# Channel mixing in five chunks of 464 tokens instead of six of 384, with results added in place

## The chip, the cores and the metric

The kernel runs on one core of a Trainium2 chip. The metric is device time in microseconds (us); the time before is the median of three runs. Engines: PE is TensorE (PEld its weight loads, which overlap with matmuls), DVE is VectorE, ACT is ScalarE, POOL is GpSimd, SP issues the transfers.

## The reference

Attention with a window of 64 comes first, then a gated spatial mixing, then a token and a channel mixing. The change touches only the last one. `_moe2_ref` is called with x of 4 x 576 x 512:

```python
def _moe2_ref(x, w_tok1, w_tok2, w_ch1, w_ch2):
    xt = x.transpose(0, 2, 1)
    h = np.maximum(xt @ w_tok1, 0.0) @ w_tok2
    u = x + h.transpose(0, 2, 1)
    h2 = np.maximum(u @ w_ch1, 0.0) @ w_ch2      # 512 -> 1536 -> 512
    return (u + h2).astype(np.float32)
```

## The kernel before

All 2,304 tokens (4 batches of 576) lie along the free axis of one tile U, 128 partitions x 4 x 2304, with the 512 features on partitions in four groups. Each product is made of three matmuls: both operands are split in a high and a low part (names ending in h and l), and high x high, high x low and low x high are summed (`mm3`, line 115 on).

The weights of both channel products come as 64-bit numbers. `load_wide` (line 93) fetches a tile into `wraw`; ACT takes a first step (line 106), DVE four (lines 107 to 111: L107, L109, L110, L111), ACT copies the high part (L112), POOL subtracts for the low part (L113). `wval` has two buffers, `wraw` three. There are 12 tiles c1 (512 x 128 each) and 12 tiles c2 (128 x 512 each). c1 of 0 to 6 and c2 of 0 to 2 are loaded while the token mixing runs; the other nine c2 and five c1 go to a pool `c2p`, which takes over memory that the token mixing uses until its end.

The token mixing runs batch by batch ahead of that: `x2nat` transposes U with PE (twenty transposes of 128 x 128 a batch, L407) into five PSUM tiles A, `tok1` makes two sums of 512 columns (hh and hl are their split, L419 and L420), `tok2` adds products of 288 columns to U (L431). PSUM has five tiles A and three tiles mm.

The channel mixing goes in chunks of CW = 384 tokens. `uin(c)` splits the chunk of U into uh (ACT, L476) and ul (DVE, L477), two buffers each. `ch1(u, ft)` makes hidden tile ft of 12: twelve matmuls of 384 columns into one mm tile (L123), then g3h (ACT, L486) and g3l (DVE, L487), four buffers each. `ch2(acc, g, ft)` adds it to four sums A, one for each output tile d, with three matmuls each (L497). ch1 is written one tile ahead of ch2. A chunk has 12 x 12 + 12 x 12 = 288 matmuls, each with a weight load. At its end DVE adds each sum and U into a tile `ot` (L532, four buffers), and SP sends it to outT (L533). The first three ch1 of chunk 0 are written between steps of the token mixing.

The order of instructions on each engine is the planner's outside the attention: it takes instructions by the order of the code and by its own estimate of when operands are ready; each engine then works its list in order.

Of the kernel before, what the change touches and what calls it, by code (L numbers as in the profile page):

```python
# [8 lines left out]
F32 = mybir.dt.float32  # L9
# [3 lines left out]
AF = mybir.ActivationFunctionType  # L13
ALU = mybir.AluOpType
# [5 lines left out]
P = 128  # L20
NTOK = B * S
# [6 lines left out]
def f(ap):  # L28
    return ap.bitcast(F32)
# [3 lines left out]
def tile_kernel(ctx, tc, qT, kT, kE, v, w_in, wsT, b_sp, w_out, w_t1, w_t2, w_c1, w_c2, mask, outT):  # L33

    nc = tc.nc

    def pool(name, side=None, stack=ctx, **kw):
        return stack.enter_context(tc.tile_pool(name=name, side=side, **kw))
# [10 lines left out]
    U = const.tile([P, 4, NTOK], F32, name="U")  # L49
# [65 lines left out]
    def mm3(o, steps, tail=()):  # L115

        todo = []
        for sh, sl, mh, ml in steps:
            todo += [(sh, mh), (sh, ml), (sl, mh)]
        todo += tail  # L120
        n = len(todo)
        for i, (a, c) in enumerate(todo):
            nc.tensor.matmul(o, a, c, start=(i == 0), stop=(i == n - 1))  # L123
# [5 lines left out]
    psmm = pool("psmm", bufs=3, space=PSUM)  # L129
# [234 lines left out]
    psA = pool("psA", bufs=5, space=PSUM)  # L364
# [69 lines left out]
    c1, c2 = {}, {}  # L434

    def load_c1(pl, ft):

        c1[ft] = [pl.tile([P, 4, 128], F32R, name=f"c1{x}{ft}") for x in "hl"]
        load_wide(lw, *[t.rearrange("p k c -> p (k c)") for t in c1[ft]],
                  w_c1[:, 128 * ft:128 * ft + 128].rearrange("(k p) c -> p k c", p=P), wmax=wmax)  # L440
# [26 lines left out]
    p3 = pool("p3", "left", stack=c_stack, bufs=1)  # L467
    wmax = DM
    lw = pool("lw3", "left", stack=c_stack, bufs=1)
    CW = 384  # L470

    def uin(c):
        t0 = CW * c
        uh = p3.tile([P, 4, CW], F32R, tag="uh", name="uh", bufs=2)
        ul = p3.tile([P, 4, CW], F32R, tag="ul", name="ul", bufs=2)
        nc.scalar.copy(out=uh, in_=U[:, :, t0:t0 + CW])  # L476
        nc.vector.tensor_tensor(out=ul, in0=U[:, :, t0:t0 + CW], in1=f(uh), op=ALU.subtract)  # L477
        return uh, ul

    def ch1(u, ft):  # L480
        uh, ul = u
        ps = psmm.tile([P, 512], F32, tag="mm", name="mm")
        mm3(ps[:, :CW], [(c1[ft][0][:, k, :], c1[ft][1][:, k, :], uh[:, k, :], ul[:, k, :]) for k in range(4)])
        gh = p3.tile([P, CW], F32R, tag="g3h", name="g3h", bufs=4)
        gl = p3.tile([P, CW], F32R, tag="g3l", name="g3l", bufs=4)
        nc.scalar.activation(out=gh, in_=ps[:, :CW], func=AF.Relu)  # L486
        nc.vector.scalar_tensor_tensor(out=gl, in0=ps[:, :CW], scalar=0.0, in1=f(gh), op0=ALU.max, op1=ALU.subtract)  # L487
        return gh, gl

    def ch2(acc, g, ft):  # L490
        gh, gl = g
        for d in range(4):
            dc = slice(128 * d, 128 * d + 128)
            wh, wl = c2[ft]
            todo = [(wh[:, dc], gh), (wl[:, dc], gh), (wh[:, dc], gl)]
            for i, (a, c) in enumerate(todo):
                nc.tensor.matmul(acc[d][:, :CW], a, c, start=(ft == 0 and i == 0), stop=(ft == 11 and i == 2))  # L497

    u0 = uin(0)
    tok2(1)  # L500
    tok1(2)
    x2nat(3)
    g0 = [ch1(u0, ft) for ft in range(2)]
    tok2(2)
    load_c1(p3, 4)
# [4 lines left out]
    load_c2(p3, 2)  # L510
    load_c1(p3, 6)
    g0.append(ch1(u0, 2))
    tok2(3)
    t_stack.close()
    r_stack.close()
    c2p = pool("c2p", "right", bufs=1)
    load_c2(c2p, 3)
    for k in range(4, 12):
        load_c2(c2p, k)
        if k < 9:  # L520
            load_c1(c2p, k + 3)
    for c in range(NTOK // CW):
        u = uin(c) if c else u0
        acc = [psA.tile([P, 512], F32, tag="A", name="A") for _ in range(4)]
        gq = [] if c else g0
        for ft in range(12):
            while len(gq) < min(ft + 2, 12):
                gq.append(ch1(u, len(gq)))
            ch2(acc, gq[ft], ft)
        for d in range(4):  # L530
            ot = c2p.tile([P, CW], F32, tag="ot", name="ot", bufs=4)
            nc.vector.tensor_tensor(out=ot, in0=acc[d][:, :CW], in1=U[:, d, CW * c:CW * c + CW], op=ALU.add)  # L532
            nc.sync.dma_start(out=outT[128 * d:128 * d + 128, CW * c:CW * c + CW], in_=ot)  # L533
    c_stack.close()


# [57 lines left out]
```

## Time and profile before

| what | value |
|---|---|
| median of three runs | 702.94 us (702.53 to 703.41) |
| the profiled execution, its own time | 704.92 us |
| its span, first to last instruction | 703.1 us |
| PE busy | 657.1 us, 93% of the span, 4,744 matmuls |
| DVE / ACT / POOL busy | 347.8 / 252.6 / 129.6 us |
| mean granted clock of PE | 0.982 |

The span is what lies between the core's first and last instruction; the execution's own time lies 1.8 us above it. Busy times are unions of records. A matmul's record overlaps with the next one's, so how fast matmuls follow each other is read from start times and counts.

### The profile page before, as it was taken

How to read it: one execution, taken by the hardware profiler on the slowest of the kernel's cores; microseconds unless marked ns; L12 is line 12 of the kernel's file. 1: busy time of each engine (PE TensorE's matmuls, PEld its weight loads, DVE VectorE, ACT ScalarE, POOL GpSimd, SP SyncE). 2: the span in 40 equal slices, each digit the busy share in tenths (PEclk: the TensorE clock that was granted, in tenths of full speed). 3: DMA queues.
4: the chain of work that ended last, by engine and by line, in shares of the span. 5: the costliest groups of instructions: out<-in, count | busy, mean ns of one | idle time of the engine just before them, and what ended most of it. 6: DMA issues, size and time to landing. Idle time of an engine off the chain costs nothing.

```text
span 703.1 us, 11915 instructions
## 1 busy us (share of the span) xinstructions
PE 657.1 (93%) x4744; PEld 627.7 (89%) x4744; DVE 347.8 (49%) x912; ACT 252.6 (36%) x675; POOL 129.6 (18%) x134
## 2 busy tenths in 40 slices
PE   2398899999999998899999998999999999999997
PEld 2387799899989898799998996999999999999996
DVE  4977576645574589921369689701311312212112
ACT  3667672553664353642345154301211111111110
POOL 2534410101220173632012143300000000000000
PEclk8589999999999999999999999999999999999999
DMA  8626552322240034100042234100100100100001
GB/s 287 199 78 186 182 170 69 116 90 68 84 151 2 1 104 129 60 1 1 1 150 91 89 121 150 45 1 1 46 1 0 46 1 1 46 0 13 34 1 45
DMA packets 27286, 50.24 MB, mean 71 GB/s; under 512 B 2784, under 2 KB 13408, under 8 KB 27232
## 3 DMA queue, kind: packets, MB, share of 16 engines
q1 hardware_dynamic: 27232, 49.49, 22.2%
q8 instruction: 37, 0.61, 0.4%
q14 instruction: 17, 0.14, 0.1%
HBM read 44.76 MB, written 4.72 MB: 70 GB/s over the span
## 4 chain that ended last, share of the span: by engine, by line
PE 75%; DVE 11%; DMA 6%; ACT 3%; issue 2%; POOL 1%; SPq 1%; DVEq 0%; POOLq 0%; ACTq 0%
PE mm L123 44%; PE A L497 20%; PE sc L184 3%; DVE wval L110 3%; PE A L123 3%; DMA kk<-in_kT 2%; PE xo L225 2%; DVE wval L111 2%; PE pt L213 2%; ACT pb L199 2%; DVE wval L107 1%; DMA raw<-in_wsT 1%; DMA U<-in_w_in 1%; DVE wval L109 1%; SPq L157 1%
## 5 line engine op out<-in xcount | busy, mean ns | idle before, releaser
L487 DVE SCALAR_TENSOR_TENSOR g3l<-mm,g3h 128x384 fp32r<-128x384 f32 x72 | 40.0, 557 | 191.0 <-ACT g3h L486 191.0
L486 ACT ACTIVATE g3h<-mm 128x384 fp32r<-128x384 f32 x72 | 35.3, 493 | 220.2 <-PE mm L123 220.1
L123 PE MATMUL mm<-uh,c1h 128*128 128x384 f32 x288 | 97.0, 337 | 1.2 <-ACT c1h L112 1.2
L497 PE MATMUL A<-g3h,c2l 128*128 128x384 f32 x288 | 97.2, 338 | 0.8 <-POOL c2l L113 0.8
L123 PE MATMUL mm<-uh,c1l 128*128 128x384 f32 x288 | 96.8, 337 | 1.2 <-POOL c1l L113 1.2
L123 PE MATMUL mm<-ul,c1h 128*128 128x384 f32 x288 | 96.7, 336 | 0.0
L497 PE MATMUL A<-g3l,c2h 128*128 128x384 f32 x288 | 94.1, 337 | 0.0
L497 PE MATMUL A<-g3h,c2h 128*128 128x384 f32 x288 | 93.7, 338 | 0.0
L199 ACT ACTIVATE pb<-pb,nm 128x128 f32<-128x128 f32 x144 | 55.9, 391 | 16.8 <-DVE nm L197 13.9
L184 PE MATMUL sc<-kk,QZ 128*64 128x128 f32 x576 | 39.7, 297 | 22.5 <-DMA kk<-in_kT 16.3
L184 PEld LDWEIGHTS sc<-kk,QZ 128*64 128x64 f32 x576 | 35.8, 152 | 23.2 <-issue 21.6
L123 PEld LDWEIGHTS mm<-uh,c1h 128*128 128x128 f32 x288 | 54.0, 188 | 1.9 <-ACT c1h L112 1.9
L123 PEld LDWEIGHTS mm<-uh,c1l 128*128 128x128 f32 x288 | 54.0, 188 | 1.9 <-POOL c1l L113 1.9
L497 PEld LDWEIGHTS A<-g3h,c2l 128*128 128x128 f32 x288 | 54.0, 187 | 1.5 <-POOL c2l L113 1.4
L497 PEld LDWEIGHTS A<-g3h,c2h 128*128 128x128 f32 x288 | 53.6, 187 | 0.6 <-ACT c2h L112 0.5
L123 PEld LDWEIGHTS mm<-ul,c1h 128*128 128x128 f32 x288 | 54.0, 188 | 0.0
L497 PEld LDWEIGHTS A<-g3l,c2h 128*128 128x128 f32 x288 | 53.8, 188 | 0.0
L123 PE MATMUL mm<-ws_h,nh 128*128 128x288 f32 x160 | 47.3, 300 | 1.9 <-DVE tmp L301 1.7
L123 PE MATMUL mm<-ws_l,nh 128*128 128x288 f32 x160 | 46.5, 295 | 0.0
L123 PE MATMUL mm<-gh,wo_h 128*128 128x288 f32 x128 | 38.2, 301 | 1.0 <-DVE tmp L301 0.8
L123 PE MATMUL mm<-gl,wo_h 128*128 128x288 f32 x128 | 38.1, 298 | 0.6 <-POOL gl L388 0.4
L194 DVE CUSTOM_DVE_ANT_0 pb<-sc,msk 128x128 f32<-128x128 f32 x144 | 33.4, 283 | 9.3 <-PE sc L184 9.3
(111 smaller groups left out, 1433.0 us busy)
## 6 DMA issues: line engine op xcount, KB each, us to landing
wraw<-in_w_c SPq DMA_DIRECT2D x24, 512.0 KB, 3.5
kk<-in_kT SPq DMA_DIRECT2D x16, 384.0 KB, 4.2
QZ<-in_qT SPq DMA_DIRECT2D x36, 128.0 KB, 4.1
va<-in_v SPq DMA_DIRECT2D x18, 256.0 KB, 3.1
vb<-in_v SPq DMA_DIRECT2D x18, 256.0 KB, 4.0
outT<-ot SPq DMA_DIRECT2D x24, 192.0 KB, 2.0
U<-in_w_in SPq DMA_DIRECT2D x8, 512.0 KB, 5.6
raw<-in_w_out SPq DMA_DIRECT2D x8, 256.0 KB, 3.6
```

The costliest lines, as they stand in the source:

```text
L107: nc.vector.tensor_scalar(out=x, in0=x, scalar1=TINY, scalar2=None, op0=ALU.max)
L110: nc.vector.scalar_tensor_tensor(out=xi, in0=high, scalar=-0x40000000, in1=xi, op0=ALU.bitwise_and, op1=ALU.bitwise_or)
L111: nc.vector.scalar_tensor_tensor(out=xi, in0=low, scalar=29, in1=xi, op0=ALU.logical_shift_right, op1=ALU.bitwise_or)
L123: nc.tensor.matmul(o, a, c, start=(i == 0), stop=(i == n - 1))
L184: nc.tensor.matmul(sc[64 * q:64 * q + 64, h, :], qz[:, h % 2, j, 64 * q:64 * q + 64], kk[:, j, step * q:step * q + 128], start=True, stop= ...
L194: nc.vector.tensor_tensor_reduce(out=half[:, h, :], in0=scs[g][:, h, :], in1=mk, scale=1.0, scalar=-3e38, op0=ALU.add, op1=ALU.max, accum_ ...
L199: nc.scalar.activation(out=half[:, h, :], in_=half[:, h, :], func=AF.Exp, scale=SCALE, bias=nm[:, h:h + 1], accum_out=sm[:, h:h + 1])
L213: nc.tensor.transpose(pt[:, h, :], pb[:, 4 * g + h, :], ident)
L225: nc.tensor.matmul(xo[64 * e:64 * e + 64, j, 64 * q:64 * q + 64], vt[q][:, hc], PT[:, 2 * j + e, 64 * q:64 * q + 64], start=True, stop=True)
L486: nc.scalar.activation(out=gh, in_=ps[:, :CW], func=AF.Relu)
L487: nc.vector.scalar_tensor_tensor(out=gl, in0=ps[:, :CW], scalar=0.0, in1=f(gh), op0=ALU.max, op1=ALU.subtract)
L497: nc.tensor.matmul(acc[d][:, :CW], a, c, start=(ft == 0 and i == 0), stop=(ft == 11 and i == 2))
```

## The change

CW becomes 464, so the 2,304 tokens fall into four chunks of 464 and one of 448; tiles are cut to a chunk's width w. A chunk's sums are added to U in place and sent from U, and the tiles `ot` go. In the last chunk, the products of the last three hidden tiles (9 to 11) are written after the others, output tile by output tile, each followed by its add and its transfer. Everything else is as it was.

```diff
-    CW = 384
+    CW = 464
 
     def uin(c):
         t0 = CW * c
+        w = min(CW, NTOK - t0)
         uh = p3.tile([P, 4, CW], F32R, tag="uh", name="uh", bufs=2)
         ul = p3.tile([P, 4, CW], F32R, tag="ul", name="ul", bufs=2)
-        nc.scalar.copy(out=uh, in_=U[:, :, t0:t0 + CW])
-        nc.vector.tensor_tensor(out=ul, in0=U[:, :, t0:t0 + CW], in1=f(uh), op=ALU.subtract)
+        uh, ul = uh[:, :, :w], ul[:, :, :w]
+        nc.scalar.copy(out=uh, in_=U[:, :, t0:t0 + w])
+        nc.vector.tensor_tensor(out=ul, in0=U[:, :, t0:t0 + w], in1=f(uh), op=ALU.subtract)
         return uh, ul
...
-    def ch2(acc, g, ft):
+    def ch2(acc, g, ft, ds=range(4)):
         gh, gl = g
-        for d in range(4):
+        for d in ds:
...
-    for c in range(NTOK // CW):
+    chunks = range(-(-NTOK // CW))
+    for c in chunks:
         u = uin(c) if c else u0
-        acc = [psA.tile([P, 512], F32, tag="A", name="A") for _ in range(4)]
+        w = u[0].shape[-1]
+        acc = [psA.tile([P, 512], F32, tag="A", name="A")[:, :w] for _ in range(4)]
         gq = [] if c else g0
+
+        late = 9 if c == chunks[-1] else 12
         for ft in range(12):
             while len(gq) < min(ft + 2, 12):
                 gq.append(ch1(u, len(gq)))
-            ch2(acc, gq[ft], ft)
+            if ft < late:
+                ch2(acc, gq[ft], ft)
         for d in range(4):
-            ot = c2p.tile([P, CW], F32, tag="ot", name="ot", bufs=4)
-            nc.vector.tensor_tensor(out=ot, in0=acc[d][:, :CW], in1=U[:, d, CW * c:CW * c + CW], op=ALU.add)
-            nc.sync.dma_start(out=outT[128 * d:128 * d + 128, CW * c:CW * c + CW], in_=ot)
+            for ft in range(late, 12):
+                ch2(acc, gq[ft], ft, (d,))
+            ts_ = slice(CW * c, CW * c + w)
+            nc.vector.tensor_tensor(out=U[:, d, ts_], in0=acc[d], in1=U[:, d, ts_], op=ALU.add)
+            nc.sync.dma_start(out=outT[128 * d:128 * d + 128, ts_], in_=U[:, d, ts_])
```

The widths make the planner place some instructions otherwise. Three places follow; the numbers behind names tell tiles of one name apart.

DVE near the end of tok1(2) (hl are its two tiles' low parts, nl the parts of natural tokens, wval the widening of weights, ul_52xx that of chunk 1). Before:

```order
L110 SCALAR_TENSOR_TENSOR wval_4600<-wraw_4599,wval_4600 128x512
L107 TENSOR_SCALAR wval_4612<-wval_4612 128x512
L431 TENSOR_TENSOR U_67<-mm_4347,U_67 128x288
L111 SCALAR_TENSOR_TENSOR wval_4600<-wraw_4599,wval_4600 128x512
L109 TENSOR_SCALAR wval_4612<-wval_4612 128x512
L477 TENSOR_TENSOR ul_5213<-U_67,uh_5212 128x1536
L420 SCALAR_TENSOR_TENSOR hl_4371<-A_4355,hh_4370 128x512
L110 SCALAR_TENSOR_TENSOR wval_4612<-wraw_4611,wval_4612 128x512
L420 SCALAR_TENSOR_TENSOR hl_4390<-A_4374,hh_4389 128x512
```

On the same engine and at the same place now:

```order
L110 SCALAR_TENSOR_TENSOR wval_4600<-wraw_4599,wval_4600 128x512
L257 TENSOR_TENSOR nl_4399<-A_4393,nh_4398 128x512
L107 TENSOR_SCALAR wval_4612<-wval_4612 128x512
L431 TENSOR_TENSOR U_67<-mm_4347,U_67 128x288
L111 SCALAR_TENSOR_TENSOR wval_4600<-wraw_4599,wval_4600 128x512
L257 TENSOR_TENSOR nl_4408<-A_4402,nh_4407 128x512
L420 SCALAR_TENSOR_TENSOR hl_4371<-A_4355,hh_4370 128x512
L109 TENSOR_SCALAR wval_4612<-wval_4612 128x512
L420 SCALAR_TENSOR_TENSOR hl_4390<-A_4374,hh_4389 128x512
L257 TENSOR_TENSOR nl_4417<-A_4411,nh_4416 128x512
L479 TENSOR_TENSOR ul_5209<-U_67,uh_5208 128x1856
```

The ul of chunk 1 stood ahead of both hl and stands behind both; two nl moved ahead of them.

DVE in the first chunk, around the widening of c1's last tile (wval_4854). Before:

```order
L111 SCALAR_TENSOR_TENSOR wval_4842<-wraw_4841,wval_4842 128x512
L107 TENSOR_SCALAR wval_4854<-wval_4854 128x512
L109 TENSOR_SCALAR wval_4854<-wval_4854 128x512
L110 SCALAR_TENSOR_TENSOR wval_4854<-wraw_4853,wval_4854 128x512
L487 SCALAR_TENSOR_TENSOR g3l_5144<-mm_5130,g3h_5143 128x384
L111 SCALAR_TENSOR_TENSOR wval_4854<-wraw_4853,wval_4854 128x512
```

On the same engine now:

```order
L491 SCALAR_TENSOR_TENSOR g3l_5086<-mm_5072,g3h_5085 128x464
L110 SCALAR_TENSOR_TENSOR wval_4842<-wraw_4841,wval_4842 128x512
L111 SCALAR_TENSOR_TENSOR wval_4842<-wraw_4841,wval_4842 128x512
L107 TENSOR_SCALAR wval_4854<-wval_4854 128x512
L109 TENSOR_SCALAR wval_4854<-wval_4854 128x512
L110 SCALAR_TENSOR_TENSOR wval_4854<-wraw_4853,wval_4854 128x512
L111 SCALAR_TENSOR_TENSOR wval_4854<-wraw_4853,wval_4854 128x512
L491 SCALAR_TENSOR_TENSOR g3l_5115<-mm_5101,g3h_5114 128x464
```

The g3l of hidden tile 10 (5144) stood ahead of the last c1 tile's last step; now those of tiles 8 and 9 (5086, 5115) stand around its steps. From hidden tile 3 on, eight g3l stood ahead of that step, and six do now.

PE's last instructions (A_6688 to A_6691 are the four sums of the last chunk before). Before:

```order
L497 MATMUL A_6688<-g3h_7012,c2h11_4887 128x384
L497 MATMUL A_6688<-g3h_7012,c2l11_4888 128x384
L497 MATMUL A_6689<-g3h_7012,c2h11_4887 128x384
L497 MATMUL A_6689<-g3h_7012,c2l11_4888 128x384
L497 MATMUL A_6690<-g3h_7012,c2h11_4887 128x384
L497 MATMUL A_6690<-g3h_7012,c2l11_4888 128x384
L497 MATMUL A_6691<-g3h_7012,c2h11_4887 128x384
L497 MATMUL A_6691<-g3h_7012,c2l11_4888 128x384
L497 MATMUL A_6688<-g3l_7013,c2h11_4887 128x384
L497 MATMUL A_6689<-g3l_7013,c2h11_4887 128x384
L497 MATMUL A_6690<-g3l_7013,c2h11_4887 128x384
L497 MATMUL A_6691<-g3l_7013,c2h11_4887 128x384
```

PE's last instructions now (A_6304 to A_6307 are the sums):

```order
L501 MATMUL A_6304<-g3h_6616,c2l11_4888 128x448
L501 MATMUL A_6305<-g3h_6616,c2h11_4887 128x448
L501 MATMUL A_6304<-g3l_6617,c2h11_4887 128x448
L501 MATMUL A_6305<-g3h_6616,c2l11_4888 128x448
L501 MATMUL A_6305<-g3l_6617,c2h11_4887 128x448
L501 MATMUL A_6306<-g3h_6616,c2h11_4887 128x448
L501 MATMUL A_6306<-g3h_6616,c2l11_4888 128x448
L501 MATMUL A_6306<-g3l_6617,c2h11_4887 128x448
L501 MATMUL A_6307<-g3l_6600,c2h10_4875 128x448
L501 MATMUL A_6307<-g3h_6616,c2h11_4887 128x448
L501 MATMUL A_6307<-g3h_6616,c2l11_4888 128x448
L501 MATMUL A_6307<-g3l_6617,c2h11_4887 128x448
```

The four sums ended in the last four matmuls; they now end with the tenth, eighth, fifth and first matmul from the end. Hidden tile 11 still comes last for all four output tiles.

## Rows read from the trace of the kernel before

**Rows 1.** The page: span, engines' busy times, and forty slices of the span.

```profile
span 703.1 us, 11915 instructions
...
PE 657.1 (93%) x4744; PEld 627.7 (89%) x4744; DVE 347.8 (49%) x912; ACT 252.6 (36%) x675; POOL 129.6 (18%) x134
...
PE   2398899999999998899999998999999999999997
...
PEclk8589999999999999999999999999999999999999
```

**Rows 2.** The chain that ended last: start us, us, engine, tile, line, count.

```profile
300.45 7.96 PE mm L123 x60
308.41 3.20 PE A L123 x14
...
498.07 4.16 PE mm L123 x24
502.23 2.08 PE A L497 x12
...
533.93 2.12 PE A L497 x12
...
653.67 2.08 PE A L497 x12
```

**Rows 3.** Stretches: length, busy us (count) of PE, PEld, DVE, ACT, POOL; PEclk, DMA, GB/s.

```profile
410.00:420.00 10.00, 10.00 (x59) 10.00 (x58) 8.08 (x14) 5.13 (x9) 5.19 (x4) 1.00 0.49 160
420.00:430.00 10.00, 8.51 (x45) 7.32 (x43) 9.83 (x15) 4.87 (x8) 3.34 (x3) 1.00 0.50 155
430.00:440.00 10.00, 8.25 (x42) 7.07 (x43) 9.72 (x14) 4.25 (x7) 3.85 (x3) 1.00 0.49 159
...
402.58:436.92 34.34, 31.10 (x169) 28.72 (x167) 29.83 (x47) 17.10 (x29) 13.91 (x10) 1.00 0.39 123
423.63:437.20 13.57, 10.33 (x50) 7.95 (x50) 13.23 (x20) 6.19 (x10) 4.87 (x5) 1.00 0.48 152
```

**Rows 4.** Timeline of PE in the first chunk: start us, us, instruction, [idle before, releaser].

```profile
430.01 0.44 PE L123 MATMUL mm<-uh,c1h 128*128 128x384 f32 x1 [0.60 <-ACT c1h L112]
...
436.92 0.44 PE L123 MATMUL mm<-uh,c1h 128*128 128x384 f32 x1 [0.61 <-ACT c1h L112]
```

**Rows 5.** Timelines of PE and of DVE around the last transposes.

```profile
373.02 0.66 PE L407 MATMUL A<-ident,U 128*128 128x128 f32 x4 [0.29 <-DVE hl L420]
375.03 0.66 PE L407 MATMUL A<-ident,U 128*128 128x128 f32 x4 [0.95 <-DVE hl L420]
...
370.62 1.75 DVE L477 TENSOR_TENSOR ul<-U,uh 128x1536 fp32r<-128x1536 f32 x1
372.28 0.68 DVE L420 SCALAR_TENSOR_TENSOR hl<-A,hh 128x512 fp32r<-128x512 f32 x1
```

**Rows 6.** Timeline of the tail, and one stretch of the table behind it.

```profile
697.22 0.87 PE L497 MATMUL A<-g3l,c2h 128*128 128x384 f32 x4
697.59 1.95 DVE L532 TENSOR_TENSOR ot<-A,U 128x384 f32<-128x384 f32 x4 [2.63 <-PE A L497]
698.18 1.80 SPq L533 DMA_DIRECT2D outT<-ot  x4
...
699.50:700.00 0.50, 0.00 (x0) 0.00 (x0) 0.04 (x1) 0.00 (x0) 0.00 (x0) 1.00 1.03 363
```

**Rows 7.** Waits: who waited for whom, us in total, times, longest (340:460, then 403:447).

```profile
ACT c2h L112 <- PE mm L123: 9.0, 1, 9.0
...
DVE g3l L487 <- ACT g3h L486: 3.6, 3, 2.2
```

**Rows 8.** Timeline of DVE in the first chunk, two weight tiles in a row.

```profile
435.07 0.55 DVE L487 SCALAR_TENSOR_TENSOR g3l<-mm,g3h 128x384 fp32r<-128x384 f32 x1
...
439.42 0.42 DVE L107 TENSOR_SCALAR wval<-wval 128x512 f32<-128x512 f32 x1
...
...
442.72 0.42 DVE L107 TENSOR_SCALAR wval<-wval 128x512 f32<-128x512 f32 x1
```

More of the change, by code (lines that the diff above doesn't have):

```diff
@@ L481, in ch1 @@
         uh, ul = u
-        ps = psmm.tile([P, 512], F32, tag="mm", name="mm")
-        mm3(ps[:, :CW], [(c1[ft][0][:, k, :], c1[ft][1][:, k, :], uh[:, k, :], ul[:, k, :]) for k in range(4)])
+        w = uh.shape[-1]
+        ps = psmm.tile([P, 512], F32, tag="mm", name="mm")[:, :w]
+        mm3(ps, [(c1[ft][0][:, k, :], c1[ft][1][:, k, :], uh[:, k, :], ul[:, k, :]) for k in range(4)])
         gh = p3.tile([P, CW], F32R, tag="g3h", name="g3h", bufs=4)
         gl = p3.tile([P, CW], F32R, tag="g3l", name="g3l", bufs=4)
-        nc.scalar.activation(out=gh, in_=ps[:, :CW], func=AF.Relu)
-        nc.vector.scalar_tensor_tensor(out=gl, in0=ps[:, :CW], scalar=0.0, in1=f(gh), op0=ALU.max, op1=ALU.subtract)
+        gh, gl = gh[:, :w], gl[:, :w]
+        nc.scalar.activation(out=gh, in_=ps, func=AF.Relu)
+        nc.vector.scalar_tensor_tensor(out=gl, in0=ps, scalar=0.0, in1=f(gh), op0=ALU.max, op1=ALU.subtract)
         return gh, gl
-    def ch2(acc, g, ft):
+    def ch2(acc, g, ft, ds=range(4)):
         gh, gl = g
-        for d in range(4):
+        for d in ds:
             dc = slice(128 * d, 128 * d + 128)
@@ L496, in ch2 @@
             for i, (a, c) in enumerate(todo):
-                nc.tensor.matmul(acc[d][:, :CW], a, c, start=(ft == 0 and i == 0), stop=(ft == 11 and i == 2))
+                nc.tensor.matmul(acc[d], a, c, start=(ft == 0 and i == 0), stop=(ft == 11 and i == 2))
     u0 = uin(0)
```

## The prediction

> **What bounds the kernel now.** I read the page's busy lines and slices first [rows 1]: TensorE (PE) is busy 657.1 of 703.1 us, and from the twenty-sixth slice to the last it stands at 9 or more nearly everywhere, at the full granted clock. The channel mixing that the change touches is 1,728 matmuls of 384 columns, six chunks of 288, and in its last two thirds nothing waits: three whole chunks lie between 502.23 and 653.67 us, so a chunk takes 50.48 us and a matmul 50.48 / 288 = 175.3 ns from start to start [rows 2]. (The 337 ns of a record overlap with the next one; the spacing is what counts.) So there the time is the number of matmuls times their spacing. The second view is the table by stretches around the first chunk [rows 3] and PE's timeline there [rows 4]: PE starts only 45 and 42 matmuls in the two stretches of 10 us from 420 on, against 59 before them; VectorE (DVE), which widens the weights, is busy 9.83 and 9.72 of 10. There the first chunk waits for its own weights. Third, before that, the four transposes that wait for hl [rows 5]; and last the tail behind the last matmul [rows 6]. Four places, four terms.
>
> **Term 1, the spacing of the matmuls.** Six chunks become four of 464 columns and one of 448: 5 x 288 = 1,440 matmuls instead of 1,728, with the same columns in sum. The gain is the part of a matmul's spacing that doesn't grow with columns. Rows at other widths give it [rows 2]: 288 columns 7.96 / 60 = 132.7 ns, 512 columns 3.20 / 14 = 228.6 ns. The slope is 95.9 / 224 = 0.428 ns a column, so some 9.4 ns are fixed on that line. From 175.3 ns at 384, 80 more columns give 175.3 + 34.2 = 209.5 ns, and 64 give 202.7. Before: 1,728 x 175.3 = 302.9 us. After: 1,152 x 209.5 + 288 x 202.7 = 241.3 + 58.4 = 299.7. Between the channel mixing's own 175.3 and the 228.6 of 512 the slope is 0.416, and 1,440 matmuls come to 298.3. The same shape runs at 173.3 ns in some groups and at 176.7 in others (12 in 2.08 or 2.12 us) [rows 2]; were all 464-column ones of the slower kind the gain would fall by about 0.4 x 3.4 x 1,440 = 2.0 us. I take -2.9 us, between -1.2 and -4.6.
>
> The Trainium skill (TensorE: Matmul & The Clock Gate, section Back-to-back issue gap) gives a spacing of columns over 2.4 GHz plus 2.5 ns. By that, term 1 would be 288 x 2.5 = 0.7 us. This trace disagrees: at a granted clock of 1.00 the spacing of 288 columns is 12.7 ns above its 120 ns of streaming, and at 512 it is 15.3 ns above 213.3 [rows 2].
>
> **Term 2, the first chunk's wait for weights.** The widening of twelve weight tiles (c1 of tile 7 to c2 of tile 11) starts when PE ends the last tok2 product: ScalarE's copy of c2 waits 9.0 us for it, to 402.58, because its tile takes over memory that is in use until then [rows 7]. From there a tile takes DVE 3.30 us (439.42 to 442.72 between two like steps) [rows 8], whatever PE does. The 72 matmuls of chunk 0 that stand ahead of this point delay it and PE alike, so they cancel. Behind it, 169 matmuls start up to 436.92, where PE waits for weights the last time [rows 3, 4]. Lost time: from 423.63 to 437.20 PE starts 50 matmuls in 13.57 us, and 13.57 - 50 x 0.1753 = 4.8 us. In the changed kernel the same weights have 169 longer matmuls in front of them: 169 x (209.5 - 175.3) = 5.8 us more work. What does it do to the weights? g3l grows from 0.55 us at 384 columns towards the 0.68 of a like operation at 512, so by 0.08 at 464 [rows 5, 8]; but the new order puts six g3l in front of c1's last tile where eight stood, so they come between 0.9 us earlier and 0.6 later. 4.8 + 0.6 - 5.8 is below zero: the wait is covered, by matmuls that had to be done anyway. I take 4.4 of the 4.8, since a wait for a single tile can stay (c2's last lo part lies beside a ul that is now longer); between -2.5 and -4.8.
>
> **Term 3, the transposes.** PE sits idle 0.29 + 0.95 = 1.24 us for two hl, and with the refill behind it about 1.8 [rows 5]. Ahead of them DVE does the ul of chunk 1, 1.75 us, at 370.62. The order now puts both hl ahead of it. It also puts nl's there and makes both ul a fifth longer (1.75 x 1856 / 1536 = 2.11). I take -0.8, between +0.5 and -1.8.
>
> **Term 4, the tail.** The last matmul starts at 697.22 + 3 x 0.175 = 697.74; the four g3l products stand last, so all four sums end together, and the four adds run one behind the other from 697.59 to 699.54 [rows 6], 1.80 us behind the last matmul's start. The new order is not tile by tile as the code reads, but it ends with four products of the last tile, 4 x 0.20 = 0.8 us, in which the third add (0.49 us at 384, about 0.56 at 448) fits. The last add then ends 697.59 - 697.22 + 0.56 = 0.93 us behind its matmul: -0.87. The last transfer is a sixth larger; four of 192 KB move at 363 GB/s, so this costs 0.1. I take -0.75, between -0.3 and -0.9.
>
> **What costs nothing.** The add in place is the same DVE operation with another target; U's columns of a chunk have no later reader but the transfer, and no wait is added. At a switch of chunks DVE does four adds (2.2 us in place of 1.95) while PE does 24 matmuls of the next chunk (4.16 us, then 5.0) [rows 2]; without that cover a switch would cost about 0.3 us, four times 1.2. SP's queue does not change order.
>
> Sum: -2.9 - 4.4 - 0.8 - 0.75 = -8.85 us. The profiled execution took 704.92 us, 1.8 more than its span of 703.1; the runs' median is 702.94. The span should be near 694.3, its execution near 696.1, and the median 702.94 - 8.85 = 694.1.
>
> **The rivals.** *Spacing in proportion to columns.* 175.3 / 384 x 464 = 211.8 ns: term 1 is nothing, the others stay, 697.0 us. For it: from 384 to 512 the spacing rises nearly so (233.7 expected, 228.6 found). Against: at 512 it is still 5 ns short. The Trainium skill's rule above lies near this case.
>
> *The weights slip with PE.* DVE's queue holds g3l, each behind PE's ch1 of the same tile; ch1 now comes every 12 x 0.2095 = 2.5 us, 0.4 later each time. Eight such steps of 0.4 + 0.08 would push the weights by 3.9 us and leave that much wait: 698.0. For it: DVE waits for ScalarE's g3h three times, 3.6 us [rows 7]. Against: from 420 to 440 DVE hardly idles, PE does.
>
> *The tail does not change.* The order still goes weight tile by weight tile; if the adds pile up as before, term 4 is nothing: 694.9.
>
> *A collision at the new width, and slower.* The two spacings of one shape, 173.3 and 176.7, show that placement matters [rows 2]. All chunk tiles move, and rows of 1,856 bytes replace 1,536. It decides once a matmul costs 8.85 / 1,440 = 6.1 ns more than I take, 215.6 ns at 464; at twice that, 221.7, the median is 702.94 + 8.8 = 711.7. Against: the observed difference is 3.4 ns, and no row of any width lies that far off the line.
>
> **How the numbers follow.** Forecast 0.66; proportional spacing 0.10; weights that slip 0.10; an unchanged tail 0.10; collision 0.04. The lower end takes most of the best bounds, -4.6 - 4.8 - 1.8 - 0.9 = -12.1, or 690.8, less 0.7 since they hardly all meet: 691.5. The upper end takes in both rivals at 697 and 698: 698.0. About 0.2% can be told from no change here; every case but the last is beyond it, save for several of them together: faster 0.94, same 0.02, slower 0.04.
>
> **What would show it.** After: chunks of 60.3 us; no idle row of PE over 0.3 us between 420 and 445; DVE's last add under 1.1 us behind the last matmul's start; the last eight of the twenty transposes ahead of tok1(3) with under 0.5 us of wait. Wrong it would be if chunks take over 61 us (term 1), if PE still starts fewer than 46 matmuls in 10 us around 430 (term 2), or if a wait for U or for PSUM comes up that no row of before has.

## The result, and the profile after

| | before | changed |
|---|---|---|
| median | 703.39 us, 6 runs | 697.43 us, 6 runs (695.68 to 700.26) |
| ratio | | 0.991, interval 0.9883 to 0.9937 |
| profiled execution, span | 704.92 us, 703.1 us | 695.76 us, 694.0 us |
| matmuls, PE busy | 4,744, 657.1 us | 4,456, 654.9 us |

The kernel is faster by 0.9%, and the interval of the ratio leaves out 1. The forecast was 694.1 in a range from 691.5 to 698.0; the median lies inside, 3.3 us above the point, and nearer to the 697.0 and 698.0 of two rivals than to it. So the median alone doesn't tell the forecast from them; the profiles have to. Two numbers stand for the size of the change, 6.0 us by the medians and 9.1 by the spans, and neither is the change alone. The attention, which it does not touch, takes a different time in each execution. A mark divides the two parts: the row of 60 products of w_out in the chain, which starts at 300.45 us before [rows 2] and here at 298.95. In the ten profiles of this study, all of them programs with the same instructions in the same order up to the mark, it lies between 297.38 and 301.81 us. From the mark to the end it is 703.1 - 300.45 = 402.65 us before and 694.0 - 298.95 = 395.05 after: 7.6 us, and two executions of the changed kernel differ there by 0.4 (395.05 and 394.66). This stretch is used below, under the name "the rest".

The page of the changed kernel, as in [rows 1]:

```profile
span 694.0 us, 11267 instructions
...
PE 654.9 (94%) x4456; PEld 595.6 (86%) x4456; DVE 346.6 (50%) x895; ACT 249.9 (36%) x662; POOL 129.4 (19%) x134
...
PE   2498899999999998899999998999999999999997
...
PEclk9789999999999999999999999999999999999999
```

The chain of the changed kernel, as in [rows 2] (start us, us, engine, tile, line, count):

```profile
298.95 7.96 PE mm L123 x60
306.91 3.21 PE A L123 x14
...
517.38 2.51 PE A L501 x12
520.30 2.56 PE A L501 x12
...
578.03 2.51 PE A L501 x12
...
643.73 2.43 PE mm L123 x12
...
677.74 4.86 PE mm L123 x24
```

The products outside the channel mixing keep their pace (7.96 us for 60). A chunk of 464 takes 578.03 - 517.38 = 60.65 us, 210.6 ns a matmul. The chunk of 448 has 168 matmuls between 643.73 and 677.74: 202.4 ns. So the channel mixing's matmuls take 1,152 x 210.6 + 288 x 202.4 ns = 300.9 us, where they took 302.9.

The stretches of the first chunk, as in [rows 3] (busy us and counts of PE, PEld, DVE, ACT, POOL):

```profile
420.00:430.00 10.00, 10.00 (x50) 8.92 (x49) 8.38 (x13) 4.81 (x9) 4.07 (x3) 1.00 0.50 157
430.00:440.00 10.00, 9.94 (x46) 8.20 (x45) 9.83 (x14) 4.34 (x8) 3.87 (x3) 1.00 0.46 144
```

PE is busy 10.00 and 9.94 of 10 us, where it was 8.51 and 8.25, and its weights come no faster than before: DVE still stands at 9.83 in the second stretch. The longest wait that is left lies at the chunk's end. ScalarE's copy of c2, POOL's low part of c1's last tile, then DVE, POOL and PE at that wait (timelines):

```profile
402.78 1.14 ACT L112 CAST c2h<-wval 128x512 fp32r<-128x512 f32 x2 [10.00 <-PE mm L123]
...
438.46 1.30 POOL L113 TENSOR_TENSOR c1l<-wval,c1h 128x512 fp32r<-128x512 f32 x1 [2.00 <-ACT c1h L112]
...
448.99 2.08 DVE L479 TENSOR_TENSOR ul<-U,uh 128x1856 fp32r<-128x1856 f32 x1
...
449.25 2.96 POOL L113 TENSOR_TENSOR c2l<-wval,c2h 128x512 fp32r<-128x512 f32 x1 [2.01 <-ACT c2h L112]
...
452.27 0.48 PE L501 MATMUL A<-g3h,c2l 128*128 128x464 f32 x1 [0.27 <-POOL c2l L113]
```

The same two low parts in the kernel before, and the ul beside the second:

```profile
436.94 1.29 POOL L113 TENSOR_TENSOR c1l<-wval,c1h 128x512 fp32r<-128x512 f32 x1 [2.34 <-ACT c1h L112]
...
446.95 1.75 DVE L477 TENSOR_TENSOR ul<-U,uh 128x1536 fp32r<-128x1536 f32 x1
...
447.06 2.79 POOL L113 TENSOR_TENSOR c2l<-wval,c2h 128x512 fp32r<-128x512 f32 x1 [2.23 <-ACT c2h L112]
```

The first row of the changed kernel is the gate of [rows 7], now at 402.78. Its last three are the wait that the prediction named as the one that could stay: POOL makes the last low part beside the ul of chunk 2, in 2.96 us, where it took 1.29 for the tile before it. That stretch is not new, though. POOL took 2.79 us for the same tile beside the shorter ul before, and PE did not wait there, its last wait being the one at 436.92 [rows 4].

Counted from the gate, c1's last low part ends at 438.23 - 402.58 = 35.65 us before and at 439.76 - 402.78 = 36.98 after, and c2's last one at 47.27 and 49.43. So the weights come 1.3 and 2.2 us later than before, and it is the longer matmuls ahead of them that cover the wait, not an earlier arrival.

DVE and PE at the transposes, as in [rows 5], and the tail, as in [rows 6], with its last add by itself:

```profile
369.01 0.68 DVE L420 SCALAR_TENSOR_TENSOR hl<-A,hh 128x512 fp32r<-128x512 f32 x1
...
369.94 0.68 DVE L420 SCALAR_TENSOR_TENSOR hl<-A,hh 128x512 fp32r<-128x512 f32 x1
...
371.14 2.93 DVE L479 TENSOR_TENSOR ul<-U,uh 128x1856 fp32r<-128x1856 f32 x1
...
372.37 0.60 PE L407 MATMUL A<-ident,U 128*128 128x128 f32 x4
...
688.11 2.45 DVE L543 TENSOR_TENSOR U<-A,U 128x448 f32<-128x448 f32 x4 [4.27 <-PE A L501]
688.76 2.15 SPq L544 DMA_DIRECT2D outT<-U  x4
...
689.53 0.37 PE L501 MATMUL A<-g3l,c2h 128*128 128x448 f32 x1
...
689.93 0.62 DVE L543 TENSOR_TENSOR U<-A,U 128x448 f32<-128x448 f32 x1
```

Both hl are done before the ul starts, and no transpose waits for one any more. In the tail the last matmul starts at 689.53 and the last add ends at 688.11 + 2.45 = 690.56, 1.03 us behind it (1.80 before). From the last matmul's start to the end of the span it is 4.47 us; before it was 703.1 - 697.74 = 5.36.

These rows divide the 7.6 us by the prediction's own terms:

- Mark to gate: 402.58 - 300.45 = 102.13 us before, 103.83 after, +1.70. The 72 longer matmuls ahead of the gate cost 72 x 35.3 ns = 2.54, so 0.84 is saved: **term 3**.
- Gate to the last matmul's start: 295.16 us before, 286.75 after. Before, 1,656 matmuls at 175.3 ns are 290.30, so 4.86 were waiting. After, 1,080 at 210.6 and 288 at 202.4 are 285.74: 1.01 us of waiting. **Term 2** is -3.85.
- All matmuls: 302.9 to 300.9, **term 1** -2.0.
- Tail: 5.36 to 4.47, **term 4** -0.89.

Together -7.6; the stretches are divided so that the terms must add up to it. From the gate to the last matmul the time repeats well: 286.76 us in the changed kernel's second execution, and 295.15 for 295.16 in the run below with chunks of 384. From mark to gate the same two have 103.47 for 103.83 and 101.86 for 102.13, so term 3 is known to some 0.3 us. That is the account; whether the causes are the ones named is what the experiments ask.

### The profile page after: what moved, and what is told of

It reads as the page before. It is cut to its first block, busy times and chain, and to the rows that moved or that the text cites. A ratio compares the mean times of both kernels' runs of the same rounds, so it can differ in the third digit from the quotient of the medians.

```text
span 694.0 us, 11267 instructions
## 1 busy us (share of the span) xinstructions
PE 654.9 (94%) x4456; PEld 595.6 (86%) x4456; DVE 346.6 (50%) x895; ACT 249.9 (36%) x662; POOL 129.4 (19%) x134
## 4 chain that ended last, share of the span: by engine, by line
PE 68%; DVE 17%; DMA 4%; issue 3%; ACT 3%; POOL 2%; SPq 1%; POOLq 0%
PE mm L123 40%; PE A L501 18%; PE sc L184 4%; DVE wval L110 4%; DVE wval L111 3%; DVE wval L107 2%; DMA kk<-in_kT 2%; PE pt L213 2%; PE A L123 2%; PE xo L225 2%; DVE wval L109 2%; DVE val L79 1%; DMA U<-in_w_in 1%; ACT wval L106 1%; DVE nl L257 1%
## 5 line engine op out<-in xcount | busy, mean ns | idle before, releaser
L491 DVE SCALAR_TENSOR_TENSOR g3l<-mm,g3h 128x464 fp32r<-128x464 f32 (+1 forms) x60 | 38.1, 635 | 178.6 <-ACT g3h L490 178.6
L490 ACT ACTIVATE g3h<-mm 128x464 fp32r<-128x464 f32 (+1 forms) x60 | 33.3, 555 | 207.9 <-PE mm L123 207.9
L501 PE MATMUL A<-g3h,c2l 128*128 128x464 f32 (+1 forms) x240 | 89.4, 372 | 0.3 <-POOL c2l L113 0.3
L123 PE MATMUL mm<-uh,c1h 128*128 128x464 f32 (+1 forms) x240 | 89.3, 372 | 0.1
L123 PE MATMUL mm<-uh,c1l 128*128 128x464 f32 (+1 forms) x240 | 89.1, 371 | 0.0
L123 PE MATMUL mm<-ul,c1h 128*128 128x464 f32 (+1 forms) x240 | 88.9, 371 | 0.0
L501 PE MATMUL A<-g3l,c2h 128*128 128x464 f32 (+1 forms) x240 | 87.1, 371 | 0.0
L501 PE MATMUL A<-g3h,c2h 128*128 128x464 f32 (+1 forms) x240 | 86.1, 371 | 0.0
L501 PEld LDWEIGHTS A<-g3h,c2l 128*128 128x128 f32 x240 | 45.0, 187 | 6.5 <-POOL c2l L113 1.5
L123 PE MATMUL mm<-ws_h,nl 128*128 128x288 f32 x128 | 37.8, 295 | 0.0
```

The source lines that it names most:

```text
L490: nc.scalar.activation(out=gh, in_=ps, func=AF.Relu)
L491: nc.vector.scalar_tensor_tensor(out=gl, in0=ps, scalar=0.0, in1=f(gh), op0=ALU.max, op1=ALU.subtract)
L501: nc.tensor.matmul(acc[d], a, c, start=(ft == 0 and i == 0), stop=(ft == 11 and i == 2))
```

## The experiments

Before each run the rivals were: the gain of the first chunk comes from its width; it comes from fewer matmuls or from the adds in place; the weights slip with PE. In the expectations the rest is counted from the first of the 60 matmuls, 0.17 us ahead of the chain's row, hence 402.8 and 395.2 for what is 402.65 and 395.05 here. All runs but the two with a shortened widening write the chunks as a list of widths, WS; its other lines stand in the run with five widths and are three dots elsewhere.

### The last products in the old order

```diff
-    CW = 464
+    WS = [464, 464, 464, 464, 448]
...
-        late = 9 if c == chunks[-1] else 12
+        late = 12 if c == chunks[-1] else 12
```

> Chunks of 464 and adds in place, but the last chunk's products written like all others. If the order of the last products gives the tail's gain: the last add ends again some 1.8 us behind the last matmul's start, where the changed kernel has 1.03, and the time is 0.9 us over its 697.43. If the tail came from the adds in place instead: no difference. Chunks stay at 60.65 us in both.

Measured: 697.2 us (695.4 to 698.78, 4 runs), ratio to before 0.9908 (0.9873 to 0.9943); the rest 396.22 us, 1.2 more than the changed kernel. The medians can't tell 0.9 us; the tail's rows can (DVE and PE timelines of this kernel):

```profile
687.34 0.99 PE L502 MATMUL A<-g3l,c2h 128*128 128x448 f32 x4
687.75 2.22 DVE L544 TENSOR_TENSOR U<-A,U 128x448 f32<-128x448 f32 x4 [3.07 <-PE A L502]
```

Again the four low products stand last and the adds pile up: the last one ends at 689.97, 2.02 us behind the last matmul's start at 687.34 + 3 x 0.202 = 687.95. The whole tail is 5.65 us. So the order makes it, and not the adds in place: with adds in place and the old order the tail is longer than before, by the larger adds.

### Six chunks of 384 with the other two edits

```diff
-    CW = 464
+    WS = [384, 384, 384, 384, 384, 384]
...
```

The adds in place and the order of the last products stay as changed.

> Six chunks of 384 as before, but with the adds in place and the last products by output tile. If width makes the gain, this keeps chunks of 50.5 us and the 4.8 us of waiting in the first chunk, and only the tail shrinks: 0.9 us under before. If the adds in place made a difference at the switches of chunks: chunks shorter than 50.5 us and more than 1.5 us under before.

Measured: 702.83 us (10 runs), ratio 0.9982 (0.996 to 1.0003); the rest 401.45 us, 1.2 under before. The tail is 4.44 us, 0.9 less than before. A chunk's matmuls stand at 175.3 ns and the waiting in the first chunk is as it was (a stretch, and the last wait of PE):

```profile
420.00:430.00 10.00, 7.87 (x40) 6.34 (x38) 9.79 (x16) 4.43 (x8) 3.78 (x3) 1.00 0.46 140
...
435.65 0.44 PE L123 MATMUL mm<-uh,c1h 128*128 128x384 f32 x1 [0.61 <-ACT c1h L112]
```

So the width carries all but the tail. The remaining 0.3 us lies between mark and gate, where this kernel and the one before run the same instructions; from gate to last matmul it takes 295.15 us, before 295.16. The adds in place are worth nothing that can be seen.

### Spacing at five widths

```diff
-    CW = 464
+    WS = [464, 440, 472, 448, 480]
+    TS = [sum(WS[:i]) for i in range(len(WS))]
+    CW = max(WS)
```

> Five chunks of 464, 440, 472, 448 and 480 tokens, to read the spacing of matmuls at five widths in one execution. If spacing is one line over width (9.4 ns and 0.428 ns a column, plus 1.5 that channel mixing had over the other 384-column products): 440 columns 199, 448 202.7, 464 209.5, 472 213, 480 216.4 ns. If it is placement rather than width that put 464 at 210.6 in the changed kernel and 448 at 202.4: the values leave the line by up to 3 ns, and 464 no longer lies above it. In proportion to columns (0.456 ns): 201, 204.5, 211.8, 215.4, 219.

Measured, one execution: 695.36 us, the rest 394.80. Rows of its chain, two from each of the last four chunks:

```profile
461.76 2.40 PE mm L123 x12
...
500.13 2.40 PE mm L123 x12
...
520.09 2.55 PE mm L123 x12
...
555.90 2.58 PE mm L123 x12
...
580.91 2.43 PE mm L123 x12
...
619.68 2.44 PE mm L123 x12
...
639.93 2.62 PE mm L123 x12
...
671.21 2.61 PE mm L123 x12
```

Between the two rows of a chunk start 192, 168, 192 and 144 matmuls, so one takes 199.8, 213.2, 201.9 and 217.2 ns. Averaged over all matmuls of a width, it is 199.8 ns at 440 columns, 202.2 at 448, 210.4 at 464, 213.1 at 472 and 216.9 at 480. The line expected 199.3, 202.7, 209.5, 213 and 216.4. All lie within 1.1 ns of it, and the proportional spacing (201 to 219) is 1.2 to 2.3 ns too high at every width. 464 columns are the value furthest above the line, both as the first chunk here and in the four chunks of the changed kernel. Part of that is the line: its slope comes from other products, of 288 and 512 columns. Between the channel mixing's own 384 and the 512 of the next run (231.5 ns) it is 0.439 ns a column, and on that line 464 stands at 210.4, while 448, 472 and 480 lie 0.5 to 1.2 ns below it. What is left over is open: neither placement nor width alone was held still.

### A first chunk of 512, four of 448

```diff
-    CW = 464
+    WS = [512, 448, 448, 448, 448]
...
```

> A first chunk of 512 tokens and four of 448. If a matmul's spacing has a fixed part that does not depend on placement: 1,152 x 202.4 + 288 x 229 ns = 299.1 us of channel mixing where the changed kernel has 1,152 x 210.6 + 288 x 202.4 = 300.9, and the weights of the first chunk have still more work in front of them, so about 2 us under the changed kernel, 695.5. If 202.4 belonged to the last chunk and not to 448 columns: 697.4, no difference.

Measured: 695.73 us (693.32 to 698.96, 4 runs), ratio 0.9891 (0.9845 to 0.9936); the rest 394.19 us, 0.9 under the changed kernel and 0.5 under its second execution. The chunks of 448 run at 202.7 ns, so this spacing belongs to the width and not to the last chunk. But 512 columns take 231.5 ns here and not 229, and PE loses about 2 us to waits in the first chunk, more than the 1.0 of the changed kernel. The two longest:

```profile
440.87 0.73 PE L502 MATMUL A<-g3l,c2h 128*128 128x512 f32 x2 [0.41 <-DVE g3l L492]
...
447.25 0.50 PE L502 MATMUL A<-g3l,c2h 128*128 128x512 f32 x1 [0.66 <-DVE g3l L492]
```

PE waits there for a g3l and not for a weight: DVE makes both, in one list, and a g3l stands behind steps of the widening. So a wider first chunk covers the weights only as long as DVE's list does not make PE wait for something else. The expected 2 us come to less than one, and the medians can't tell this kernel from the changed one.

### A narrow first chunk and four wide ones

```diff
-    CW = 464
+    WS = [384, 480, 480, 480, 480]
...
```

> A first chunk of 384 tokens and four of 480: as few matmuls as the changed kernel, but the first chunk is no wider than before, and the planner again puts the ul of chunk 1 ahead of both hl. If the first chunk's width is what covers the weights: some 5 us of PE waiting behind the last tok2 product come back, and 1.5 us or more at the transposes; term 1 is worth 302.9 - (288 x 175.3 + 1,152 x 216.9 ns = 300.4) = 2.5 us, the tail 0.9, so from the start of batch 1's first product of w_out to the end it takes 402.8 - 3.4 = 399.4 us (before 402.8, changed kernel 395.2), and the time is near 700. If the waits went because of fewer matmuls or adds in place: 395 and 697.

This is the run that tells the first two rivals apart: 1,440 matmuls, adds in place, the new order of the last products, and only the first chunk as narrow as before (the planner's order around it turns back with it). Measured: 701.16 us (10 runs), ratio 0.9953 (0.9929 to 0.9977); the rest 399.23 us, where 399.4 was worked out and 395 was the rival's. Its timeline of PE in the first chunk, and the transposes:

```profile
372.77 0.66 PE L407 MATMUL A<-ident,U 128*128 128x128 f32 x4 [0.86 <-DVE hl L420]
...
429.16 0.44 PE L123 MATMUL mm<-uh,c1h 128*128 128x384 f32 x1 [0.61 <-ACT c1h L112]
430.51 0.44 PE L123 MATMUL mm<-uh,c1l 128*128 128x384 f32 x1 [0.74 <-POOL c1l L113]
...
436.07 0.44 PE L123 MATMUL mm<-uh,c1h 128*128 128x384 f32 x1 [0.58 <-ACT c1h L112]
```

The waits of [rows 4] are back with nearly the same lengths (0.61 and 0.58 for 0.60 and 0.61), and the transpose waits for hl again, since this width made the planner put the ul ahead of hl. In the stretches from 420 on PE starts 41 and 40 matmuls. Five chunks without a wide first one are worth 3.4 us, with one 7.6.

### The weights' widening cut short, before and changed

```diff
         nc.vector.tensor_scalar(out=x, in0=x, scalar1=TINY, scalar2=None, op0=ALU.max)
         xi = x.bitcast(I32)
-        nc.vector.tensor_scalar(out=xi, in0=xi, scalar1=0x07FFFFFF, scalar2=3, op0=ALU.bitwise_and, op1=ALU.logical_shift_left)
-        nc.vector.scalar_tensor_tensor(out=xi, in0=high, scalar=-0x40000000, in1=xi, op0=ALU.bitwise_and, op1=ALU.bitwise_or)
-        nc.vector.scalar_tensor_tensor(out=xi, in0=low, scalar=29, in1=xi, op0=ALU.logical_shift_right, op1=ALU.bitwise_or)
+        if wmax != DM:
+            nc.vector.tensor_scalar(out=xi, in0=xi, scalar1=0x07FFFFFF, scalar2=3, op0=ALU.bitwise_and, op1=ALU.logical_shift_left)
+            nc.vector.scalar_tensor_tensor(out=xi, in0=high, scalar=-0x40000000, in1=xi, op0=ALU.bitwise_and, op1=ALU.bitwise_or)
+            nc.vector.scalar_tensor_tensor(out=xi, in0=low, scalar=29, in1=xi, op0=ALU.logical_shift_right, op1=ALU.bitwise_or)
```

> The kernel before, with three of the four steps of DVE left out when the last twenty weight tiles of the channel mixing are widened (so its output is not the reference's). If DVE's widening makes PE wait in the first chunk: the 5 us of PE waiting behind the last tok2 product are gone, and with them the 1.5 us or so at the transposes; from the first product of w_out of batch 1 to the end 402.8 - 6.5 = 396.3 us. If the transfers of the weights or ACT and POOL set the pace: less than 2 us of it.

Measured, one execution: 697.06 us, the rest 395.79 us, 6.9 under before (expected 6.5). The two stretches of the first chunk:

```profile
420.00:430.00 10.00, 10.00 (x59) 10.00 (x58) 4.53 (x8) 5.97 (x11) 5.97 (x5) 1.00 0.22 74
430.00:440.00 10.00, 10.00 (x59) 10.00 (x58) 4.25 (x6) 1.85 (x2) 0.00 (x0) 1.00 0.00 0
```

PE starts 59 matmuls in each and DVE is busy 4.53 and 4.25. With three DVE steps gone the waiting is gone, though the transfers, ACT's and POOL's parts are all there: DVE set the pace. What DVE loses beside POOL goes with the steps (the last section has its rows), so this run doesn't tell DVE's own work from that.

> The changed kernel with the same three steps left out for the same tiles (its output is not the reference's). If the change's width has already covered the weights: only the 1.35 us of waiting that are left there can go, 395.2 - 1.4 = 393.8 us for the same stretch, so the two shortened kernels differ by terms 1 and 4 alone, 2.0 + 0.9 = 2.9 us, where the two full ones differ by 7.6. If the weights had merely slipped with PE: 3 us or more gained, and a difference nearer to 7.

Measured, one execution: 695.63 us, the rest 393.15 us, 1.9 under the changed kernel. The same two stretches:

```profile
420.00:430.00 10.00, 10.00 (x48) 8.51 (x47) 5.61 (x7) 5.66 (x11) 5.94 (x5) 1.00 0.60 188
430.00:440.00 10.00, 10.00 (x49) 8.91 (x49) 2.01 (x5) 3.36 (x6) 2.56 (x3) 1.00 0.01 2
```

So the widening costs the kernel before 6.9 us and the changed one 1.9: the wide first chunk covers 5.0 of it, which is terms 2 and 3 (3.85 + 0.84 = 4.7) seen from the other side. The two shortened kernels differ by 2.64 us, where terms 1 and 4 make 2.9. A slip of the weights as large as the rival's would have left 3 us or more to gain here; the slip of 1.3 to 2.2 us that the low parts show can cost at most these 1.9.

### The changed kernel once more

```diff
-    CW = 464
+    WS = [464, 464, 464, 464, 448]
...
```

> The changed kernel again, with its chunks written as a list of widths (the same instructions in the same order), to narrow its ratio to before. If the profiled executions tell the change's size (7.6 us in the part that it can touch): 703.4 - 7.6 = 695.8. If the median of its first six runs does: 697.4.

Measured: 697.09 us (694.45 to 699.97, 6 runs), ratio to before 0.9897 (0.9861 to 0.9934); the rest 394.66. The median came out as in the first six, against the first of the two expectations, but the runs of before beside it had a median of 704.68, so the difference is 7.6 here and 6.0 there. (The last four runs were on another chip than the four ahead of them; each ratio is to the runs of before beside it.) Over the three sets of runs before has 36 with a median of 703.8 and a standard deviation of 1.7 us, the changed kernel 12 with 697.4 and 1.8. The difference is 6.4 us by these medians and 6.9 by the means, with a standard error of 0.6; the rest in the profiles gives 7.6, which two executions repeat to 0.4. The two agree within their errors.

## Why the prediction was right, point by point

**What bounds the kernel** was read rightly. Each of the four places gave something. That the terms add up to the rest proves nothing, as they were divided to do so; what bears them out is the runs. The signs that the prediction named came too: chunks of 60.65 us, no idle row of PE over 0.3 us between 420 and 445, no transpose that waits for hl, and a last add 1.03 us behind its matmul.

**Term 1** was taken at 2.9 us and came to 2.0. The step that was off is the spacing of 464 columns: 209.5 ns with the slope of the products of 288 and 512 columns, 210.6 measured. One nanosecond on 1,152 matmuls is 1.3 us. The channel mixing's own slope, 0.439 ns a column by the run with 512, would have given 1.9. The 448-column chunk gave back 0.1 (202.7 and 202.4). The value lies inside the bounds that were named, 1.2 to 4.6 (redone, the slope of 0.416 gives 298.5 and not 298.3 us, so 4.4). The rule of 2.5 ns beside the streaming, that the Trainium skill states in TensorE: Matmul & The Clock Gate, section Back-to-back issue gap, is by that section the gap of an isolated matmul; the prediction took it for a stream, and it does not fit this one: at 464 columns and a granted clock of 1.00 the spacing is 17.3 ns above its 193.3 of streaming.

**Term 2** was taken at 4.4 and came to 3.85. The mechanism was right and is shown from two sides: with a first chunk of 384 the waits return, and without three DVE steps they go in the kernel before. What was mis-sized is the remainder, 1.0 us and not 0.4. The step behind it is when the weights come: the prediction had c1's last tile between 0.9 us earlier and 0.6 later, and its low part came 1.3 later, that of c2's last tile 2.2 later. With 1.3 in place of 0.6 its sum, 4.8 + 1.3 - 6.0, is no longer below zero. One place of the remainder is the one that the prediction named, POOL's last low part beside a ul, but the longer ul is hardly the reason: 2.96 us after, 2.79 before. The Trainium skill (GPSIMD Engine Reference, section 1. Specifications) says that GpSimd shares its SBUF interfaces with VectorE and contends with VectorE's instructions that have two SBUF inputs, as the ul has; this trace agrees: POOL took 2.96 us where the ul had started 0.26 us ahead of it, and 1.29 for the tile before.

**Term 3** was taken at 0.8 between a loss of 0.5 and a gain of 1.8, and came to 0.84, between 0.6 and 1.2 by the other runs of both orders. That the order of hl and ul is its cause is borne out by the kernel with a narrow first chunk, where the planner's order turned back and the wait of 0.86 us was there. It is a by-product: no line of the change asks for it, and another width can lose it.

**Term 4** was taken at 0.75 and came to 0.89. The last add ends 1.03 us behind its matmul, 0.1 later than worked out. The last add did wait for its matmul, as was said, and began 0.40 us behind it; but it took 0.62 us and not 0.56, since the 0.49 that this was scaled from is the distance of two adds in a row and not the length of one.

**The rival of proportional spacing** is refuted by the five widths. **The weights that slip** are half right: they slip by 1.3 to 2.2 us, not by 3.9, and most of it is covered, as the shortened changed kernel shows (1.9 us and not 3 or more). Whether they slip for the rival's reason is not shown. **The unchanged tail** is refuted by the tail's rows. **The collision** did not happen at its price; a piece of it, 1.1 ns at 464 columns, may be there. That placement makes the two spacings of one shape is not shown by any run.

**The sum** of 8.85 us was 1.25 too large against the 7.6 of the rest. The span came out at 694.0 where 694.3 was worked out, but that is partly luck: 1.5 us of the 9.1 were saved ahead of the mark, in the part that is not changed. The rest of the distance between 694.1 and 697.43 lies in the medians of few runs: the point was set from 702.94, the median of three, where six give 703.39 and 36 give 703.8, and the difference of the first medians, 6.0, is 1.6 us under that of the profiles.

## What to carry to other kernels

When an engine is bound by the count of its instructions, fewer and wider ones save the fixed part of each: read the spacing from starts and counts at two widths, of the same kind of product where you can, and expect the line to be off by a nanosecond. A wait for a resource that comes at its own pace can be filled by making the waiting engine's earlier work bigger, if that work must be done anyway; count how much of it stands ahead of the last wait, compare it with the time lost, and ask how much later the resource will come, since the engine that makes it gets bigger work too. Where the unchanged part of a kernel varies more than the change is worth, compare profiles from a mark at which the two programs still run the same instructions.

## What the runs showed of the hardware

- The same code ahead of the mark took 297.38 to 301.81 us in ten profiles, while behind it two executions of one kernel agreed to 0.4. The granted clock in the first 20 us was 0.80 to 0.84 in some of them and 1.00 in others, without a clear relation to that time (1.00 in the longest, 301.81 us, and 0.84 in the shortest); from 20 to 40 us it was between 0.51 and 0.78 in all ten. The cause is open.
- Where a POOL low part and a DVE operation with two SBUF inputs lay side by side, the one that started second took longer. The low part took 2.96 us where a ul of 128x1856 had started 0.26 ahead, and that ul 2.08; at 371.14 the ul took 2.93, a low part of 1.29 having started at 370.84. It also meets the widening, here in the changed kernel:

```profile
440.08 0.69 DVE L110 SCALAR_TENSOR_TENSOR wval<-wraw,wval 128x512 int32<-128x512 int32 x1
...
442.65 1.29 POOL L113 TENSOR_TENSOR c2l<-wval,c2h 128x512 fp32r<-128x512 f32 x1 [2.89 <-ACT c2h L112]
...
442.76 1.73 DVE L110 SCALAR_TENSOR_TENSOR wval<-wraw,wval 128x512 int32<-128x512 int32 x1
```

  L110 took 0.69 us by itself and 1.73 behind a low part, so an estimated 1 us of DVE's 3.30 for a tile comes from POOL.
- Matmuls of one width do not run at one spacing: 173.3 to 176.7 ns at 384 columns, 2.50 to 2.56 us for twelve of 464.
